# Deltanet with a two-expert router: 832 rows an expert in place of 896, the last 64 on the divided array

## The chip, the cores and the metric

The kernel runs on one core of a Trainium2 chip. The metric is device time in microseconds, the median of several runs. TensorE (PE) multiplies and transposes, VectorE (DVE) and ScalarE (ACT) read what it leaves in PSUM, GpSimd (POOL) issues the indirect DMAs, and SyncE (SP) the plain ones.

## The reference

Two blocks follow one another. The first is a linear attention with a delta rule over 4 batches, 8 heads, 768 steps and 48 channels. Its result becomes 3072 rows of 384 for a mixture of 8 experts, of which each row takes two:

```python
for t in range(S):
    y[:, :, t] = einsum('bhd,bhde->bhe', q[:, :, t], state)
    v_old = einsum('bhde,bhd->bhe', state, kt)
    state = state + bt * einsum('bhd,bhe->bhde', kt, vt - v_old)
...
noisy_logits = x @ w_gate + np.log1p(np.exp(x @ w_noise)) * noise
top2 = the two largest of 8; top2_w = their softmax
for e in range(E):                       # E = 8
    h = np.maximum(x[mask] @ w1[e], 0.0) # 384 -> 1024
    out[mask] += top2_w * (h @ w2[e])    # 1024 -> 384
```

All inputs and outputs are float32. Counted from the reference on its inputs, the eight experts get 711, 771, 789, 774, 756, 744, 807 and 792 rows.

## The kernel before

The deltanet stage routes as it goes. For every token it writes one row of 388 numbers (384 of x, and the token's number, gates and expert) twice into `rows_x`, a buffer in HBM with one part for each expert, by indirect DMAs of GpSimd (`spread`, L176). Ahead of that SP clears the first 896 rows of each part (`clear`, L171) to rows that carry the number of no token. `before` holds the running counts of rows per expert.

The expert stage takes each expert in turn (loop at L794), always with TILES = 7 tiles of 128 rows:

- SP loads all seven tiles as one DMA into `xr` (L798; two buffers, so the next expert's rows come early) and then the weights of the next expert.
- VectorE takes the token numbers and gates out of `xr` (L806, L760, L764).
- GpSimd gathers the sums so far of these tokens from the output into `sums` (L776), which waits for the scatters of the expert before.
- TensorE transposes each tile (three 128*128 transposes, L733), and VectorE copies them to `xe` (L734).
- `first` multiplies with w1: two halves of 448 rows as moving columns, eight blocks of F, three steps of the contraction each (L740), and ScalarE evicts with a Relu (L744).
- `second` multiplies tile by tile with w2: eight blocks of F accumulate 384 columns in one PSUM bank (L750). VectorE multiplies by the gate and adds to `sums` (L754), and GpSimd scatters the tile to the output (L785).

A scheduler places the instructions on each engine from their dependences, in program order with small exchanges. PSUM buffers come from a pool of eight banks that transposes, first and second products share. A float32 matmul shows as two records in the trace, a transpose as one.

After the loop a matmul of ones with `before` gives the counts (L836), VectorE reduces them to the largest (L838, L839), all engines load it into a register (`values_load`, L840), and a branch (L841) does the left-over rows, tile by tile with 128 columns, if an expert has more than TILES * 128.

Of the kernel before, what the change touches and what calls it, by code (L numbers as in the profile page):

```python
# [8 lines left out]
FP32 = mybir.dt.float32  # L9
I32 = mybir.dt.int32  # L10
ALU = mybir.AluOpType
ACTF = mybir.ActivationFunctionType
AX = mybir.AxisListType
SYNC = mybir.DependencyInfo(mybir.DependencyClass.Sync, mybir.DependencyReason.DATA)
# [1 line left out]
C = 64  # L16
DP = 64
Q = 32
TILES = 7
ROW = 384 + 4  # L20
HALF = TILES * 128 // 2


@with_exitstack
def kernel(
# [10 lines left out]
    moe_w2: bass.AP,  # L36
    out: bass.AP,
):

# [23 lines left out]
    nc = tc.nc  # L63

    B, H, S, D = q.shape
    N, DM = out.shape
    E = moe_w_gate.shape[1]
# [7 lines left out]
    KT = DM // 128  # L75
    FT = F // 128
# [62 lines left out]
    def load_weights(pool, e):  # L139
        w1e = pool.tile([128, KT, F], FP32, name="w1e")  # L140
        w2e = pool.tile([128, FT, DM], FP32, name="w2e")
        nc.sync.dma_start(out=w1e, in_=w1r[e])
        nc.sync.dma_start(out=w2e, in_=w2r[e])
        return w1e, w2e
# [23 lines left out]
    def clear(e):  # L168

        return nc.sync.dma_start(  # L170
            out=rows_x[e * N : e * N + TILES * 128].rearrange("(t p) d -> p t d", p=128),  # L171
            in_=empty[:, None, :].to_broadcast([128, TILES, ROW]),
        ).ins

    def spread(rows, slot):
# [549 lines left out]
    def ps(shape, name):  # L725
        return psum.tile(shape, FP32, name=name, tag="ps")

    moe = ctx.enter_context(tc.tile_pool(name="moe", bufs=2))

    def transposed(xr, xe, i):  # L730
        p_xt = ps([128, KT, 128], "p_xt")
        for do in range(KT):
            nc.tensor.transpose(p_xt[:, do], xr[:, i, do * 128 : (do + 1) * 128], ident)  # L733
        nc.vector.tensor_copy(xe[:, :, i * 128 : (i + 1) * 128], p_xt)  # L734

    def first(w1e, xe, hT, cols):
        for fo in range(FT):
            p_h = ps([128, cols.stop - cols.start], "p_h")
            for do in range(KT):
                nc.tensor.matmul(  # L740
                    p_h, w1e[:, do, fo * 128 : (fo + 1) * 128], xe[:, do, cols],
                    start=(do == 0), stop=(do == KT - 1),
                )
            nc.scalar.activation(hT[:, fo, cols], p_h, ACTF.Relu)  # L744

    def second(w2e, hT, i, gate, got):

        p_o = ps([128, DM], "p_o")
        for fo in range(FT):
            nc.tensor.matmul(  # L750
                p_o, hT[:, fo, i * 128 : (i + 1) * 128], w2e[:, fo],
                start=(fo == 0), stop=(fo == FT - 1),
            )
        nc.vector.scalar_tensor_tensor(  # L754
            out=got, in0=p_o, scalar=gate, in1=got, op0=ALU.mult, op1=ALU.add
        )

    def gates_of(xr, e, gate):

        nc.vector.scalar_tensor_tensor(  # L760
            out=gate, in0=xr[:, :, DM + 3], scalar=float(e - E), in1=xr[:, :, DM + 2],
            op0=ALU.is_equal, op1=ALU.mult,
        )
        nc.vector.tensor_tensor(out=gate, in0=gate, in1=xr[:, :, DM + 1], op=ALU.add)  # L764
# [9 lines left out]
    def gather(got, index, group, earlier):  # L774
        return ordered(
            nc.gpsimd.indirect_dma_start(  # L776
                out=got, out_offset=None, in_=out,
                in_offset=bass.IndirectOffsetOnAxis(ap=index, axis=0),
                bounds_check=N - 1, oob_is_err=False,
            ).ins, group, earlier,  # L780
        )

    def scatter(got, index, group, earlier):
        return ordered(
            nc.gpsimd.indirect_dma_start(  # L785
                out=out, out_offset=bass.IndirectOffsetOnAxis(ap=index, axis=0), in_=got,
                in_offset=None, bounds_check=N - 1, oob_is_err=False,
            ).ins, group, earlier,
        )

    sums = [moe.tile([128, TILES, DM], FP32, name=f"sums{i}", bufs=1) for i in range(2)]
    for got in sums:
        nc.gpsimd.memset(got, 0.0)
    for e in range(E):  # L794
        w1e, w2e = weights
        rows = slice(e * N, e * N + TILES * 128)
        xr = moe.tile([128, TILES, ROW], FP32, name="xr")
        d = nc.sync.dma_start(  # L798
            out=xr, in_=rows_x[rows].rearrange("(t p) d -> p t d", p=128)
        ).ins  # L800
        for i in written:
            tc.add_manual_dep(d, i.name, SYNC, reason="rows of all tokens")
        if e + 1 < E:
            weights = load_weights(w_odd if e % 2 == 0 else w_even, e + 1)
        index = moe.tile([128, TILES], I32, name="index")
        nc.vector.tensor_copy(index, xr[:, :, DM])  # L806
        gate = moe.tile([128, TILES], FP32, name="gate")
        gates_of(xr, e, gate)
        got = sums[e % 2]
        gathers = [  # L810
            gather(got[:, i], index[:, i : i + 1], f"out{e}", added) for i in range(TILES)
        ]
        added = []
        xe = moe.tile([128, KT, TILES * 128], FP32, name="xe")
        for i in range(TILES):
            transposed(xr, xe, i)
        hT = moe.tile([128, FT, TILES * 128], FP32, name="hT", bufs=1)
        for h0 in range(0, TILES * 128, HALF):
            first(w1e, xe, hT, slice(h0, h0 + HALF))
        for i in range(TILES):  # L820
            second(w2e, hT, i, gate[:, i : i + 1], got[:, i])
            added.append(
                scatter(got[:, i], index[:, i : i + 1], f"out{e}", gathers if i == 0 else [])
            )


    counts = moe.tile([128, E], FP32, name="counts", bufs=1)
    most = moe.tile([128, 1], FP32, name="most", bufs=1)
    most_i = moe.tile([128, 1], I32, name="most_i", bufs=1)
    place = moe.tile([128, NT], FP32, name="place", bufs=1)  # L830
    nc.gpsimd.iota(
        place, pattern=[[128, NT]], base=0, channel_multiplier=1,
        allow_small_or_imprecise_dtypes=True,
    )
    p_n = ps([128, E], "p_n")
    nc.tensor.matmul(p_n, ones, before)  # L836
    nc.vector.tensor_copy(counts, p_n)
    nc.vector.tensor_reduce(out=most, in_=counts, axis=AX.X, op=ALU.max)  # L838
    nc.vector.tensor_copy(most_i, most)  # L839
    count = nc.values_load(most_i[0:1, 0:1], min_val=0, max_val=N)  # L840
    with tc.If(count > TILES * 128):  # L841
        for e in range(E):
            with tc.tile_pool(name=f"left{e}", bufs=1) as pool:
                w1e = pool.tile([128, KT, F], FP32, name="w1l")
                w2e = pool.tile([128, FT, DM], FP32, name="w2l")
                nc.sync.dma_start(out=w1e, in_=w1r[e])
                nc.sync.dma_start(out=w2e, in_=w2r[e])
                earlier, added = added, []
                for i in range(TILES, NT):
                    r0 = e * N + i * 128  # L850
                    xr = pool.tile([128, 1, ROW], FP32, name="xrl")
                    nc.sync.dma_start(out=xr[:, 0], in_=rows_x[r0 : r0 + 128])
# [55 lines left out]
```

## Time and profile before

| | |
|---|---|
| median of 3 runs | 1134.44 us (1134.03 to 1136.22) |
| profiled execution | 1132.78 us, span 1131.1 us |
| TensorE matmul busy | 933.2 us (83%) |
| first products L740 | 291.0 us, 768 records |
| second products L750 | 290.3 us, 896 records |
| transposes L733 | 21.9 us, 168 records |
| mean granted TensorE clock | 0.825 |

Busy times are sums over the whole span. [...] A record's own duration is longer than the step to the next one, since matmuls are pipelined; the steps tell what a matmul costs in a stream.

### The profile page before, as it was taken

Reading aid. Unit: us, or ns where it says so; the run is one execution under the profiler, and the core shown is the slowest. Engines: PE = TensorE matmul, PEld = TensorE weight load, DVE = VectorE, ACT = ScalarE, POOL = GpSimd, SP = SyncE. Lnnn points to the kernel's source line nnn. Section 1 sums busy time; section 2 is a strip of 40 time slices with the busy share of each in tenths; the row PEclk is TensorE's granted clock in tenths of the full one; section 3 lists DMA queues with packets and bytes.
Section 4 is the critical chain, followed back from the end, with each engine's and each line's share of the span. In section 5 each row is a group of like instructions: output and inputs, shape, how many; then the busy total and the mean of one; then the engine's idle time right before and its main releaser. Section 6 shows DMA issues by size and latency. Waiting matters only on the chain.

```text
span 1131.1 us, 20168 instructions
## 1 busy us (share of the span) xinstructions
PE 933.2 (83%) x8670; PEld 631.0 (56%) x8670; DVE 314.1 (28%) x883; ACT 257.4 (23%) x621; POOL 239.8 (21%) x297
## 2 busy tenths in 40 slices
PE   2258147877958688827999999999999999999995
PEld 2258046777858677724565555555655555556553
DVE  1866753383664733011010020110100201102000
ACT  3353234434416242101102002011020020110200
POOL 4201112314142140223022121130221211301211
PEclk9655558675666656558999999999999999999998
DMA  5895202322121120118114241241142412301100
GB/s 106 255 369 151 42 2 65 79 45 82 29 75 33 30 72 2 57 57 297 63 36 143 77 139 31 91 156 63 48 134 76 143 29 86 106 8 37 43 21 26
DMA packets 120403, 96.34 MB, mean 85 GB/s; under 512 B 84690, under 2 KB 110350, under 8 KB 120304
## 3 DMA queue, kind: packets, MB, share of 16 engines
q1 hardware_dynamic: 109168, 66.42, 20.1%
q0 software_dynamic: 10240, 28.43, 7.4%
q8 instruction: 70, 1.15, 0.4%
q14 instruction: 29, 0.24, 0.1%
q10 hardware_dynamic: 896, 0.10, 0.1%
HBM read 61.68 MB, written 36.39 MB: 87 GB/s over the span
## 4 chain that ended last, share of the span: by engine, by line
PE 70%; DVE 11%; issue 6%; ACT 6%; another core or an unknown queue 2%; DMA 1%; POOL 1%; ACTq 1%; SPq 0%; DVEq 0%; POOLq 0%
PE p_h L740 26%; PE p_o L750 26%; PE p_y L426 3%; DVE t L348 2%; DVE part L344 2%; PE p_y L420 2%; PE p_u L485 2%; PE p_xt L446 2%; PE p_x L388 2%; ACT w L373 2%; ACT gd L304 1%; PE p_x L379 1%; PE p_xt L438 1%; PE p_b L281 1%
## 5 line engine op out<-in xcount | busy, mean ns | idle before, releaser
L740 PE MATMUL p_h<-xe,w1e 128*128 128x448 f32 x768 | 291.0, 540 | 1.9 <-DVE xe L734 1.9
L750 PE MATMUL p_o<-w2e,hT 128*128 128x384 f32 x896 | 290.3, 486 | 0.0
L750 PEld LDWEIGHTS p_o<-w2e,hT 128*128 128x128 f32 x896 | 170.2, 190 | 119.6 <-issue 3.0
L740 PEld LDWEIGHTS p_h<-xe,w1e 128*128 128x128 f32 x768 | 145.5, 190 | 143.4 <-issue 139.9
L744 ACT ACTIVATE hT<-p_h 128x448 f32<-128x448 f32 x128 | 69.5, 543 | 520.3 <-PE p_h L740 483.2
L754 DVE SCALAR_TENSOR_TENSOR sums<-p_o,gate,sums 128x384 f32<-128x384 f32 x56 | 34.6, 617 | 508.4 <-PE p_o L750 508.4
L785 POOL DMA_INDIRECT out_dram<-sums,index x56 | 55.6, 993 | 438.6 <-DVE sums L754 428.8
L176 POOL DMA_INDIRECT rows_x<-y,slot x48 | 49.8, 1038 | 90.3 <-issue 41.2
L776 POOL DMA_INDIRECT sums<-out_dram,index x56 | 56.5, 1010 | 55.2 <-issue 38.5
L348 DVE TENSOR_TENSOR t<-t,part 128x30 f32<-128x30 f32 (+9 forms) x180 | 61.2, 340 | 4.8
L344 DVE TENSOR_TENSOR part<-t 128x30 f32<-128x30 f32 (+9 forms) x180 | 60.9, 338 | 4.8
L281 PE MATMUL p_q<-qT,kT 64*64 64x64 f32 x768 | 18.8, 256 | 51.0 <-ACT qT L273 48.9
L485 PE MATMUL p_u<-v,w 64*64 64x48 f32 x768 | 43.3, 284 | 10.3 <-ACT y L433 8.9
L373 ACT COPY w<-tt 32x256 f32<-32x256 f32 x96 | 38.6, 402 | 56.8 <-DVE tt L359 55.4
L485 PEld LDWEIGHTS p_u<-v,w 64*64 64x64 f32 x768 | 40.6, 202 | 13.8 <-ACT y L433 6.8
L281 PEld LDWEIGHTS p_q<-qT,kT 64*64 64x64 f32 x768 | 16.4, 164 | 54.7 <-ACT qT L273 52.3
L426 PE MATMUL p_y<-u,qk 64*64 64x48 f32 x768 | 45.8, 298 | 0.0
L426 PEld LDWEIGHTS p_y<-u,qk 64*64 64x64 f32 x768 | 41.9, 213 | 5.3 <-issue 4.9
L515 POOL COPY wide<-st 64x384 f32<-64x384 f32 x44 | 23.0, 523 | 98.1 <-DVE st L512 82.6
L459 POOL TENSOR_TENSOR v<-v,norms 128x384 f32<-128x384 f32 x24 | 21.1, 892 | 99.3 <-DMA v<-in_v_dram 84.4
L379 PE MATMUL p_x<-tb,at 32*32 32x32 f32 x768 | 21.8, 220 | 24.0 <-DVE tb L360 22.1
L733 PE MATMUL p_xt<-ident,xr 128*128 128x128 f32 x168 | 21.9, 291 | 20.0 <-DMA xr<-rows_x 20.0
(130 smaller groups left out, 824.3 us busy)
## 6 DMA issues: line engine op xcount, KB each, us to landing
w1e<-in_moe_w_dram SPq DMA_DIRECT2D x8, 1536.0 KB
w2e<-in_moe_w_dram SPq DMA_DIRECT2D x8, 1536.0 KB
rows_x<-empty SPq DMA_DIRECT2D x8, 1358.0 KB
xr<-rows_x SPq DMA_DIRECT2D x8, 1358.0 KB
kp<-in_k_dram SPq DMA_DIRECT2D x48, 96.0 KB
qp<-in_q_dram SPq DMA_DIRECT2D x48, 96.0 KB
v<-in_v_dram SPq DMA_DIRECT2D x48, 96.0 KB
out_dram<-empty SPq DMA_DIRECT2D x1, 4608.0 KB
```

Source lines behind the costliest of these rows:

```text
L176: d = nc.gpsimd.indirect_dma_start(out=rows_x, out_offset=bass.IndirectOffsetOnAxis(ap=slot, axis=0), in_=rows, in_offset=None,).ins
L281: nc.tensor.matmul(out[rows_of[b], z, j], lhsT[rows_of[z], j, rows_of[b]], rhs(rows_of[z], j, b), start=(j == 0), stop=(j == NP - 1), skip ...
L344: nc.vector.tensor_tensor(out=part, in0=t[:, j + 1 :, j, None].to_broadcast(shape), in1=t[:, None, j, 0:j].to_broadcast(shape), op=ALU.mult,)
L348: nc.vector.tensor_tensor(out=t[:, j + 1 :, 0:j], in0=t[:, j + 1 :, 0:j], in1=part, op=ALU.add)
L373: nc.scalar.copy(w64[rows, :, cols], tt[rows])
L426: nc.tensor.matmul(p_y[b, h], qk[b, h % 2, h // 2], u[b, h], start=(c == 0 and h == 0), stop=(h == H - 1), skip_group_check=True,)
L485: nc.tensor.matmul(p_u[b, h], w64[b, h], r[b, h], start=(h == 0), stop=(h == H - 1), skip_group_check=True,)
L740: nc.tensor.matmul(p_h, w1e[:, do, fo * 128 : (fo + 1) * 128], xe[:, do, cols], start=(do == 0), stop=(do == KT - 1),)
L744: nc.scalar.activation(hT[:, fo, cols], p_h, ACTF.Relu)
L750: nc.tensor.matmul(p_o, hT[:, fo, i * 128 : (i + 1) * 128], w2e[:, fo], start=(fo == 0), stop=(fo == FT - 1),)
L776: nc.gpsimd.indirect_dma_start(out=got, out_offset=None, in_=out, in_offset=bass.IndirectOffsetOnAxis(ap=index, axis=0), bounds_check=N - ...
L785: nc.gpsimd.indirect_dma_start(out=out, out_offset=bass.IndirectOffsetOnAxis(ap=index, axis=0), in_=got, in_offset=None, bounds_check=N - ...
```

## The change

TILES becomes 6, and 64 rows more (MORE) make 832 rows an expert. The first products take two halves of 416 columns. The seventh tile has 64 rows: its transposes read 64 partitions, and its second products load 64 columns of weights. `second_half` gives the even blocks of F to the PSUM partitions 0 to 63 and the odd ones to 64 to 127, and VectorE adds the two halves to `sums` one after the other. `xr` is loaded by two DMAs, and the numbers and gates are taken in two pieces. The count of rows stands ahead of the expert loop, and its load into registers behind expert 0. The branch for left-over rows starts at the seventh tile and leaves out its first 64 rows.

```diff
-TILES = 7
+TILES = 6
+MORE = 64
+ROWS = TILES * 128 + MORE
-HALF = TILES * 128 // 2
+HALF = ROWS // 2
...
-    def transposed(xr, xe, i):
+    def transposed(xr, xe, i, rows=128):
         p_xt = ps([128, KT, 128], "p_xt")
         for do in range(KT):
-            nc.tensor.transpose(p_xt[:, do], xr[:, i, do * 128 : (do + 1) * 128], ident)
-        nc.vector.tensor_copy(xe[:, :, i * 128 : (i + 1) * 128], p_xt)
+            nc.tensor.transpose(
+                p_xt[:, do, 0:rows], xr[0:rows, i, do * 128 : (do + 1) * 128],
+                ident[0:rows, 0:rows],
+            )
+        nc.vector.tensor_copy(xe[:, :, i * 128 : i * 128 + rows], p_xt[:, :, 0:rows])
...
+    def second_half(w2e, hT, gate, got):
+
+        p_o = ps([128, DM], "p_o")
+        halves = [slice(lo, lo + MORE) for lo in (0, 64)]
+        for fo in range(FT):
+            nc.tensor.matmul(
+                p_o[halves[fo % 2]], hT[:, fo, ROWS - MORE : ROWS], w2e[:, fo],
+                start=(fo < 2), stop=(fo >= FT - 2), skip_group_check=True,
+            )
+        for half in halves:
+            nc.vector.scalar_tensor_tensor(
+                out=got[0:MORE], in0=p_o[half], scalar=gate[0:MORE], in1=got[0:MORE],
+                op0=ALU.mult, op1=ALU.add,
+            )
...
+    p_n = ps([128, E], "p_n")
+    nc.tensor.matmul(p_n, ones, before)
+    nc.vector.tensor_copy(counts, p_n)
+    nc.vector.tensor_reduce(out=most, in_=counts, axis=AX.X, op=ALU.max)
+    nc.vector.tensor_copy(most_i, most)
...
+        loads = [
+            nc.sync.dma_start(
+                out=xr[:, 0:TILES], in_=rows_x[rows].rearrange("(t p) d -> p t d", p=128)
+            ).ins,
+            nc.sync.dma_start(out=xr[0:MORE, TILES], in_=rows_x[more]).ins,
+        ]
...
-        for i in range(TILES):
-            second(w2e, hT, i, gate[:, i : i + 1], got[:, i])
+        for i, p in enumerate(rows_in):
+            if p < 128:
+                second_half(w2e, hT, gate[:, i : i + 1], got[:, i])
+            else:
+                second(w2e, hT, i, gate[:, i : i + 1], got[:, i])
...
+        if e == 0:
+            count = nc.values_load(most_i[0:1, 0:1], min_val=0, max_val=N)
...
-    with tc.If(count > TILES * 128):
+    with tc.If(count > ROWS):
```

On TensorE the end of the deltanet stage and the first expert stood in this order before (p_xt are transposes, p_h first products, p_o second products; a row counts matmuls):

```order
L591 MATMUL p_at<-r_taken,ones 128x8
L595 MATMUL p_at<-before,ones 128x32
L733 MATMUL p_xt<-ident,xr 128x128 x21
L740 MATMUL p_h<-xe,w1e 128x448 x48
L750 MATMUL p_o<-w2e,hT 128x384 x56
```

The same three rows follow for every further expert.

The same place on TensorE now:

```order
L599 MATMUL p_at<-before,ones 128x32
L818 MATMUL p_n<-before,ones 128x8
L737 MATMUL p_xt<-ident,xr 128x128 x18
L737 MATMUL p_xt<-ident,xr 128x64 x3
L747 MATMUL p_h<-xe,w1e 128x416 x48
L772 MATMUL p_o<-w2e,hT 128x384 x48
L758 MATMUL p_o<-w2e,hT 64x384 x8
```

The counting matmul p_n has come ahead of the first transposes, and eight matmuls of 64 rows stand where eight of 128 stood, right before the next expert's transposes.

On VectorE the border between experts 0 and 1 was, before, the last sums of expert 0 and then the copies of expert 1's transposes (one p_xt for each tile):

```order
L754 SCALAR_TENSOR_TENSOR sums0_6110<-p_o_6328,gate_6122,sums0_6110 128x384
L754 SCALAR_TENSOR_TENSOR sums0_6110<-p_o_6341,gate_6122,sums0_6110 128x384
L734 COPY xe_6386<-p_xt_6387 128x3x128
L734 COPY xe_6386<-p_xt_6392 128x3x128
L734 COPY xe_6386<-p_xt_6397 128x3x128
L734 COPY xe_6386<-p_xt_6402 128x3x128
```

Three more copies follow, one for each further tile.

The same border on VectorE now, with the half tile's bank p_o_6353 read twice:

```order
L776 SCALAR_TENSOR_TENSOR sums0_6118<-p_o_6340,gate_6130,sums0_6118 128x384
L763 SCALAR_TENSOR_TENSOR sums0_6118<-p_o_6353,gate_6130,sums0_6118 64x384
L741 COPY xe_6417<-p_xt_6418 128x3x128
L763 SCALAR_TENSOR_TENSOR sums0_6118<-p_o_6353,gate_6130,sums0_6118 64x384
L741 COPY xe_6417<-p_xt_6423 128x3x128
L741 COPY xe_6417<-p_xt_6428 128x3x128
L741 COPY xe_6417<-p_xt_6433 128x3x128
```

The half tile's second sum has come between the first and the second copy.

On SP the loads of expert 0's rows and expert 1's weights, and what follows them, now read as follows (TENSOR_LOAD puts the count into a register):

```order
L833 DMA xr<-rows_x 128x6x388
L836 DMA xr<-rows_x 64x388
L146 DMA w1e<-in_moe_w_dram 128x3x1024
L147 DMA w2e<-in_moe_w_dram 128x8x384
L869 TENSOR_LOAD most_i
L869 ISA x2
```

Expert 1's rows come right behind these. Before, the load of the count stood behind all of SP's DMAs; on the four other engines it stands last before and now.

## Rows read from the trace of the kernel before

**Rows 1.** Windows: expert stage; busy us and records, clock, DMA.

```profile
core 0: us, PE busy (x) PEld busy (x) DVE busy (x) ACT busy (x) POOL busy (x), PEclk, DMA share, GB/s
...
519.30:1117.20 597.90, 595.99 (x1814) 332.38 (x1813) 60.28 (x128) 69.53 (x128) 108.55 (x109) 1.00 0.24 81
```

**Rows 2.** Windows: expert 0's transposes, a border, then first and second products.

```profile
514.74:519.80 5.06, 5.04 (x22) 4.86 (x23) 4.05 (x10) 0.00 (x0) 3.06 (x3) 0.50 1.03 394
...
591.74:594.47 2.73, 2.46 (x22) 2.22 (x21) 2.53 (x6) 0.00 (x0) 0.98 (x1) 1.00 0.54 85
594.47:630.65 36.18, 36.18 (x96) 18.35 (x97) 1.76 (x6) 8.15 (x15) 7.07 (x7) 1.00 0.33 109
630.65:666.77 36.12, 36.12 (x113) 21.23 (x112) 3.71 (x6) 0.54 (x1) 5.96 (x6) 1.00 0.21 76
```

**Rows 3.** Timeline, border of experts 0 and 1: start, us, instruction, count [idle <-releaser].

```profile
590.77 1.13 PE L750 MATMUL p_o<-w2e,hT 128*128 128x384 f32 x3
...
591.74 2.46 PE L733 MATMUL p_xt<-ident,xr 128*128 128x128 f32 x21
...
591.94 0.62 DVE L754 SCALAR_TENSOR_TENSOR sums<-p_o,gate,sums 128x384 f32<-128x384 f32 x1 [4.54 <-PE p_o L750]
592.48 3.33 DVE L734 COPY xe<-p_xt 128x384 f32<-128x384 f32 x7
...
594.47 1.77 PE L740 MATMUL p_h<-xe,w1e 128*128 128x448 f32 x4 [0.27 <-DVE xe L734]
```

**Rows 4.** Waits of TensorE: us in total, times, longest.

```profile
PE p_h L740 <- DVE xe L734: 1.9, 7, 0.3
```

**Rows 5.** Instruction groups: count, busy us, mean ns, idle before.

```profile
L750 PE MATMUL p_o<-w2e,hT 128*128 128x384 f32 x896 | 290.3, 486 | 0.0
...
L744 ACT ACTIVATE hT<-p_h 128x448 f32<-128x448 f32 x128 | 69.5, 543 | 520.3 <-PE p_h L740 483.2 <-DMA sums<-out_dram,index 30.4 <-issue 6.8
```

**Rows 6.** Timeline: products of the deltanet stage on column halves.

```profile
471.81 0.91 PE L420 MATMUL p_y<-wide,qT 128*64 128x96 f32 x8
```

**Rows 7.** Line L420 from 470 to 482: ns, min, median and max.

```profile
L420 PE MATMUL p_y<-wide,qT x32: 367/368/423, 471.8 to 481.0; 128*64 128x96 f32 x32
```

**Rows 8.** Windows: inside those L420 products, and inside 64*64 products of L281.

```profile
471.80:472.35 0.55, 0.55 (x8) 0.54 (x8) 0.00 (x0) 0.43 (x1) 0.00 (x0) 0.50 0.00 0
446.34:446.75 0.41, 0.41 (x32) 0.41 (x36) 0.38 (x2) 0.33 (x1) 0.37 (x2) 1.00 0.00 0
```

**Rows 9.** Timeline: expert 0's transposes.

```profile
514.76 4.71 PE L733 MATMUL p_xt<-ident,xr 128*128 128x128 f32 x21 [19.98 <-DMA xr<-rows_x]
```

**Rows 10.** Line L733, all transposes: ns, min, median and max.

```profile
L733 PE MATMUL p_xt<-ident,xr x168: 272/273/445, 514.8 to 1044.1; 128*128 128x128 f32 x168
```

**Rows 11.** Timeline: changes between whole and divided array at full clock.

```profile
441.65 0.55 PE L438 MATMUL p_xt<-ident,y 128*128 128x128 f32 x3
442.13 0.55 PE L503 MATMUL p_s<-u,kp 64*64 64x48 f32 x20
...
444.37 1.09 PE L271 MATMUL p_t<-ident,qp 128*128 128x128 f32 x8
```

**Rows 12.** Timeline of SP's loads at the start of the expert stage.

```profile
508.42 0.38 SPq L798 DMA_DIRECT2D xr<-rows_x  x1
...
509.98 9.88 SPq L798 DMA_DIRECT2D xr<-rows_x  x2
```

**Rows 13.** The page's DMA issues: the load of an expert's rows.

```profile
xr<-rows_x SPq DMA_DIRECT2D x8, 1358.0 KB
```

**Rows 14.** Timeline of GpSimd: the last scatter.

```profile
1118.07 0.98 POOL L785 DMA_INDIRECT out_dram<-sums,index  x1 [4.18 <-DVE most L838]
```

**Rows 15.** Window after it.

```profile
1119.10:1131.10 12.00, 0.00 (x0) 0.00 (x0) 0.00 (x0) 0.00 (x0) 0.00 (x0) 0.56 0.06 13
```

**Rows 16.** Waits of SP's queue.

```profile
SPq L840 <- DVE most_i L839: 150.4, 1, 150.4
```

**Rows 17.** Line L841, the branch, on TensorE: ns.

```profile
L841 PEldq COMPARE_BRANCH  x1: 3512/3512/3512, 1119.2 to 1119.2; - x1
```

More of the change, by code (lines that the diff above doesn't have):

```diff
@@ L170, in clear @@
         return nc.sync.dma_start(
-            out=rows_x[e * N : e * N + TILES * 128].rearrange("(t p) d -> p t d", p=128),
-            in_=empty[:, None, :].to_broadcast([128, TILES, ROW]),
+            out=rows_x[e * N : e * N + (TILES + 1) * 128].rearrange("(t p) d -> p t d", p=128),
+            in_=empty[:, None, :].to_broadcast([128, (TILES + 1), ROW]),
         ).ins
@@ L789, in scatter @@
         )
-    sums = [moe.tile([128, TILES, DM], FP32, name=f"sums{i}", bufs=1) for i in range(2)]
+    counts = moe.tile([128, E], FP32, name="counts", bufs=1)
+    most = moe.tile([128, 1], FP32, name="most", bufs=1)
+    most_i = moe.tile([128, 1], I32, name="most_i", bufs=1)
+    p_n = ps([128, E], "p_n")
[3 more added lines that the diff above has]
+    nc.vector.tensor_copy(most_i, most)
+    sums = [moe.tile([128, TILES + 1, DM], FP32, name=f"sums{i}", bufs=1) for i in range(2)]
     for got in sums:
         nc.gpsimd.memset(got, 0.0)
+    rows_in = [128] * TILES + [MORE]
     for e in range(E):
@@ L796 @@
         rows = slice(e * N, e * N + TILES * 128)
[L797 to L802, printed above, removed]
+        more = slice(rows.stop, rows.stop + MORE)
+        xr = moe.tile([128, TILES + 1, ROW], FP32, name="xr")
+        loads = [
[4 more added lines that the diff above has]
+        ]
@@ L803 @@
+        for d in loads:
+            for i in written:
+                tc.add_manual_dep(d, i.name, SYNC, reason="rows of all tokens")
         if e + 1 < E:
             weights = load_weights(w_odd if e % 2 == 0 else w_even, e + 1)
[L805 to L808, printed above, removed]
+        index = moe.tile([128, TILES + 1], I32, name="index")
+        gate = moe.tile([128, TILES + 1], FP32, name="gate")
@@ L809 @@
+        for p, t in ((128, slice(0, TILES)), (MORE, slice(TILES, TILES + 1))):
+            nc.vector.tensor_copy(index[0:p, t], xr[0:p, t, DM])
+            gates_of(xr[0:p, t], e, gate[0:p, t])
         got = sums[e % 2]
         gathers = [
-            gather(got[:, i], index[:, i : i + 1], f"out{e}", added) for i in range(TILES)
+            gather(got[0:p, i], index[0:p, i : i + 1], f"out{e}", added)
+            for i, p in enumerate(rows_in)
         ]
         added = []
-        xe = moe.tile([128, KT, TILES * 128], FP32, name="xe")
@@ L815 @@
-        for i in range(TILES):
-            transposed(xr, xe, i)
-        hT = moe.tile([128, FT, TILES * 128], FP32, name="hT", bufs=1)
-        for h0 in range(0, TILES * 128, HALF):
-            first(w1e, xe, hT, slice(h0, h0 + HALF))
-        for i in range(TILES):
-            second(w2e, hT, i, gate[:, i : i + 1], got[:, i])
+        xe = moe.tile([128, KT, ROWS], FP32, name="xe")
+        for i, p in enumerate(rows_in):
+            transposed(xr, xe, i, p)
+        hT = moe.tile([128, FT, ROWS], FP32, name="hT", bufs=1)
@@ L822 @@
+        for h0 in range(0, ROWS, HALF):
+            first(w1e, xe, hT, slice(h0, h0 + HALF))
+        for i, p in enumerate(rows_in):
+            if p < 128:
+                second_half(w2e, hT, gate[:, i : i + 1], got[:, i])
+            else:
+                second(w2e, hT, i, gate[:, i : i + 1], got[:, i])
             added.append(
-                scatter(got[:, i], index[:, i : i + 1], f"out{e}", gathers if i == 0 else [])
+                scatter(got[0:p, i], index[0:p, i : i + 1], f"out{e}", gathers if i == 0 else [])
@@ L824 @@
             )
-    counts = moe.tile([128, E], FP32, name="counts", bufs=1)
-    most = moe.tile([128, 1], FP32, name="most", bufs=1)
-    most_i = moe.tile([128, 1], I32, name="most_i", bufs=1)
+        if e == 0:
+            count = nc.values_load(most_i[0:1, 0:1], min_val=0, max_val=N)
     place = moe.tile([128, NT], FP32, name="place", bufs=1)
@@ L834 @@
     )
[L835 to L840, printed above, removed]
-    with tc.If(count > TILES * 128):
+    nc.vector.memset(place[0:MORE, TILES : TILES + 1], float(N))
+    with tc.If(count > ROWS):
         for e in range(E):
```

## The prediction

> **What bounds the kernel now.** I read the page first for where the time lies, then the windows of one expert, then the timeline of one border between two experts, and last the places where the trace already shows the forms of instruction that the change brings in. [...] One expert is three stretches [rows 2]: 36.18 us of first products (96 records, two for each of 48 matmuls), 36.12 us of second products (112 records for 56 matmuls, so 5.16 us a tile), and 2.73 us of border, in which 21 transposes run and TensorE then waits 0.27 us for VectorE (594.47 less 591.74 + 2.46), seven times in the program [rows 3]. No load, eviction or scatter ends a wait of TensorE inside the stage except 1.9 us on xe [rows 4]. So a column that goes away in L740 or L750 is time that goes away, and all else is to be counted at the borders, the start and the end.
>
> **First products.** 448 columns become 416. Per record 36.18/96 = 0.377 us, or 0.84 ns a column; the second products give 36.12/112 = 0.3225 us for 384 columns, 0.84 ns again, so time goes by columns. 36.18 x 32/448 = 2.58 us an expert, **-20.7 us** for eight. ScalarE's eviction (543 ns [rows 5]) runs once in six records (2.1 us) and stays hidden.
>
> **Second products.** Six full tiles keep their 5.16 us. The seventh has 64 rows: eight matmuls that each load 64 columns of weights and write 64 partitions, even blocks to the lower half, odd ones to the upper. The trace has this very form: L420, 128*64, whose inner loop also alternates the halves. Eight records of 96 columns take 0.91 us, the last 0.37, so (0.91 - 0.37)/7 = 0.077 us a record, at clock 0.50 [rows 6 to 8]. One after the other at that clock they would take 0.16 us: the transposes of expert 0 at clock 0.50 need (4.71 - 0.445)/20 = 0.213 us for 128 columns [rows 9, 10], 1.67 ns a column, times 96. Two therefore run at once. That this holds at the upper clock is seen in 64*64 products at clock 1.00: 32 records of 64 columns in 0.41 us, 0.013 each where 0.054 would be due alone [rows 8]; four at a time there, with the same number of partitions streamed as two of 128. So the half tile costs 16 x 0.3225/2 = 2.58 us in place of 5.16: 2.58 us an expert, **-20.6 us**. Bounds: nothing (no overlap), and the 20.6.
>
> **Change of form.** Between 128*128 and a divided array the next load begins only near the end of the last matmul. At full clock the last of three transposes starts at 441.65 + 0.55 - 0.273 = 441.93 and the 64*64 products at 442.13, 0.20 us later where the step inside one form is (2.46 - 0.273)/20 = 0.109; going back, eight transposes take 1.09 us, some 0.05 more than at 0.109 a step [rows 3, 10, 11]. So about 0.15 us a change. Four changes come with each expert: into the half tile, out of it, and into and out of the 64-row transposes. Only the first stands on the path, since the other three lie in the border, where TensorE waits for VectorE: **+1.2 us** (8 x 0.15; 0.4 to 2.8). [...]
>
> **The border.** Before, the last second product starts at 590.77 + 1.13 - 0.486 = 591.41 [rows 3, 5]; VectorE's sum follows at 591.94, the first xe copy at 592.48, the others every (3.33 - 0.55)/6 = 0.464 us, and L740 starts at 594.47, just when the fourth copy ends (592.48 + 3 x 0.464 + 0.55 = 594.42) [rows 3]. 416 columns need four tiles as well. In the new order the second sum of the half tile stands between the first and the second copy, on the path. A sum before a copy takes 0.54 us there (592.48 - 591.94), so every border grows by about 0.54 us, seven times: **+3.8 us** (0.3 to 0.9 a border). TensorE's transposes, over by some 2.9 us after the last second product, stay ahead of the copies that end at 3.6.
>
> **Start of the stage.** Expert 0's first load goes from 1,358 to 1,164 KB (six tiles of seven). TensorE starts 6.34 us after SP issues it; 194 KB at the 394 GB/s of that stretch is 0.5 us [rows 2, 9, 12, 13]. What is won runs at the lower clock if that rises when it did, at 519.8, so **-0.4 us** (0 to -0.9). VectorE has three more small operations ahead of its copies (0.17 us each), hidden because the transposes come at 0.64 us a tile there. The counting matmul and its three VectorE operations move into the 20 us in which TensorE waits for that load.
>
> **The count.** Only SP's TENSOR_LOAD moves forward, behind the loads of expert 1's weights; on the four other engines it still stands last. It waits for one VectorE cast that is early now. Behind it on SP stands expert 1's xr, issued at 509.98 before, in 9.88 us together with the next one, and used at 591.74 [rows 3, 12]: some 70 us of room, so nothing.
>
> **The end.** After the last scatter (1118.07 + 0.98) no engine works for 12.0 us [rows 14, 15]. The last expert's two sums follow one another with no copy between: the scatter comes 0.65 us later (0.618 and a wait). Against that TensorE, ScalarE and SP no longer wait for the count until 1118.3 (SP waited 150.4 us for it [rows 16]), and TensorE's branch of 3.5 us [rows 17] may run beside matmuls; but GpSimd, whose path goes through the scatter, gains little. **+0.4 us** (-0.4 to +0.7).
>
> **Sum.** -20.7 - 20.6 + 1.2 + 3.8 - 0.4 + 0.4 = -36.3 us. The profiled execution took 1132.78 us (span 1131.1): 1096.5. The median shown, 1134.44, lies 1.66 above it, so the forecast is 1098.1 us, say **1098**. With the bounds of the terms (-40 to -31) and the spread of the runs shown it is 1094 to 1104.
>
> **Rivals.**
> (a) The halves do not overlap for 384 columns, because two streams of 128 partitions are needed at the upper clock, of which L420's rows say nothing (0.50). For it: no row has this form at 1.00. Against: the 64*64 rows. The 20.6 are not won: 1118.7 us. 5%.
> (b) The clock falls at the borders. They hold 2.6 us of work on the divided array, transposes, and 0.8 us of waiting instead of 0.27. After expert 0's long wait the clock stayed at 0.50 for 5.06 us, through 21 transposes [rows 2]; if each of seven borders cost the same, 5.06 x 0.5 = 2.5 us each is 17.7 us: 1116. Against: seven borders of today keep 1.00, with 2.46 us of transposes in them. 8%. [...]
> (c) Slower: the branch for rows beyond the tiles is taken. It decides from 833 rows of one expert, where 897 were needed. Then 8 x 18 tiles of 128 rows follow, at 5.16 us for their second products alone: over 740 us more, above 1840. Against: counting the reference's routing on its inputs gives 711 to 807 rows an expert. 0.5%.
> (d) Both (a) and (b): 38.3 us lost of 36.3 won, 1136. 0.5%.
>
> **How the numbers follow.** The forecast's case has 83%, (a) 5%, (b) 8%, and 4% are left for (c), (d) and costs that I do not see. Of the first case some 3 in 83 fall outside its own range widened to 1093 to 1107, which so holds 8 in 10; (a) and (b) stay outside it. Within 0.2% (2.3 us, about what a measurement of this kernel can tell from no change) lie (d) and half of what I do not see: 2%; slower are (c) and the other half: 2%; the rest, with (a) and (b), is faster: 96%.
>
> **What would show it.** Right: L747 records every 0.349 us; L758 records in pairs that take 2.6 us an expert; a period from one expert's first product to the next of 70.6 us for 75.0; TensorE idle 0.7 to 1.0 us before L747 behind VectorE; clock 1.00 from 519 us on; the second sum between two xe copies. Wrong: L758 at 0.32 us a record one after another (a), a stretch of 0.50 inside the stage (b), any xrl instruction at all (c), or TensorE waiting for DMA at a border.

## The result, and the profile after

The changed kernel takes 1100.97 us (median of 4 runs, 1097.86 to 1106.57) where the kernel before took 1135.33 us beside it (median of 4, 1134.03 to 1139.32): a ratio of 0.970, with a 95% interval from 0.965 to 0.975. The forecast was 1098 us, in a range of 1093 to 1107. Its profiled execution took 1099.18 us with a span of 1097.5 us, 33.6 us under the span before.

First the page's costliest groups of the changed kernel: line, engine, operation, tiles and shapes, count, then busy us and mean ns of one, then the idle time before them and its releaser.

```profile
L747 PE MATMUL p_h<-xe,w1e 128*128 128x416 f32 x768 | 270.3, 513 | 6.3 <-DVE xe L741 6.3
L772 PE MATMUL p_o<-w2e,hT 128*128 128x384 f32 x768 | 249.0, 486 | 0.0
```

Six tiles of 128 rows are left for L772 (768 records for the 896 of [rows 5]), and L747 now sits idle for 6.3 us behind VectorE's xe, where [rows 4] had 1.9: three times as much, still seven times in the program.

Then the windows that answer to [rows 1, 2]: expert 0's transposes in two pieces, the expert stage from its first product to its last matmul, and of the border its transposes, of expert 1 the first products, the six tiles and the half tile. Columns as in [rows 1].

```profile
514.57:518.19 3.62, 3.60 (x17) 3.62 (x18) 3.04 (x11) 0.00 (x0) 2.06 (x3) 0.50 1.01 396
518.19:518.75 0.56, 0.56 (x6) 0.33 (x4) 0.56 (x2) 0.00 (x0) 0.56 (x1) 1.00 1.06 370
518.76:1081.90 563.14, 556.82 (x1813) 315.11 (x1811) 64.87 (x155) 66.18 (x128) 107.47 (x109) 1.00 0.26 85
...
586.16:589.58 3.42, 2.52 (x23) 2.21 (x21) 3.23 (x7) 0.00 (x0) 0.93 (x1) 1.00 0.67 182
589.58:623.21 33.63, 33.62 (x96) 18.35 (x97) 1.69 (x9) 7.75 (x15) 6.99 (x7) 1.00 0.31 104
623.21:654.26 31.05, 31.05 (x97) 18.05 (x95) 3.09 (x5) 0.52 (x1) 4.98 (x5) 1.00 0.23 83
654.26:656.99 2.73, 2.73 (x17) 1.06 (x16) 0.62 (x1) 0.00 (x0) 0.98 (x1) 1.00 0.07 27
```

First products go from 36.18 to 33.63 us an expert, second products from 36.12 to 31.05 + 2.73 = 33.78, the stretch from the first transpose to the next first product from 2.73 to 3.42 [rows 2]. The granted clock, given as a share of the full one, is 1.00 from the second row on, in the border's row too, and so from the first product to the last.

The timeline of the border between experts 0 and 1, TensorE first, then VectorE; the line of 583.81 is the second pair of the half tile's sixteen records by itself. Each line has its start, its us, the instruction with its count, and in brackets the idle time before it with the releaser.

```profile
583.02 0.49 PE L772 MATMUL p_o<-w2e,hT 128*128 128x384 f32 x1
583.44 2.80 PE L758 MATMUL p_o<-w2e,hT 128*64 128x384 f32 x16
...
583.81 0.49 PE L758 MATMUL p_o<-w2e,hT 128*64 128x384 f32 x2
...
586.17 2.51 PE L737 MATMUL p_xt<-ident,xr 128*128 128x128 f32 x21
589.59 0.62 PE L747 MATMUL p_h<-xe,w1e 128*128 128x416 f32 x1 [0.91 <-DVE xe L741]
...
586.29 0.61 DVE L763 SCALAR_TENSOR_TENSOR sums<-p_o,gate,sums 64x384 f32<-64x384 f32 x1 [2.12 <-PE p_o L758]
586.82 0.54 DVE L741 COPY xe<-p_xt 128x384 f32<-128x384 f32 x1
587.39 0.62 DVE L763 SCALAR_TENSOR_TENSOR sums<-p_o,gate,sums 64x384 f32<-64x384 f32 x1
588.04 2.42 DVE L741 COPY xe<-p_xt 128x384 f32<-128x384 f32 x5
...
660.41 0.62 PE L747 MATMUL p_h<-xe,w1e 128*128 128x416 f32 x1 [0.90 <-DVE xe L741]
```

Sixteen records of the half tile take 2.80 us where one alone takes 0.486 us. They start in pairs, one record of each half with 0.007 us between them; all fifteen steps together are 2.80 - 0.49 = 2.31 us, 0.154 us a record on average, about half of the 0.3225 us of a whole tile's [rows 2]. The last of them starts at 583.44 + 2.80 - 0.49 = 585.75 and the next expert's first product at 589.59, 3.84 us later; before, it was 594.47 - 591.41 = 3.06 [rows 3, 5]. From one expert's first product to the next it is 660.41 - 589.59 = 70.82 us, for 75.03 before. On VectorE the second half sum stands between the first and the second copy, as forecast, but the steps around it are 0.57 and 0.65 us, where 0.464 stood.

Last the end: the last half tile on TensorE, the last scatter, and what GpSimd's queue does behind the overflow branch (count, ns of one as min/median/max, start of the first and of the last).

```profile
1079.21 2.80 PE L758 MATMUL p_o<-w2e,hT 128*64 128x384 f32 x16
...
1083.61 0.92 POOL L807 DMA_INDIRECT out_dram<-sums,index  x1 [2.41 <-DVE sums L763]
...
L879 POOLq EVENT_SEMAPHORE  x4: 17/42/43, 1088.9 to 1091.2; - x4
L879 POOLq COMPARE_BRANCH  x1: 53/53/53, 1085.1 to 1085.1; - x1
...
L879 POOLq INC_SWDGE_SEM  x1: 1170/1170/1170, 1091.3 to 1091.3; - x1
```

And of the kernel before, its last second products and the same rows of GpSimd's queue:

```profile
1109.56 7.58 PE L750 MATMUL p_o<-w2e,hT 128*128 128x384 f32 x23
...
L841 POOLq EVENT_SEMAPHORE  x4: 17/43/43, 1124.1 to 1124.3; - x4
L841 POOLq COMPARE_BRANCH  x1: 53/53/53, 1119.5 to 1119.5; - x1
```

GpSimd takes its branch at 1085.1 and runs the first instruction behind it at 1088.9, 3.9 us later (before: 4.5). But then four semaphore instructions that took 0.2 us before take 2.3 us. Single records show where: 2.115 us lie between the first and the second of them, and in that gap one packet of 8192 bytes comes on an instruction queue (1089.56 to 1089.92). The last second product starts at 1079.21 + 2.80 - 0.49 = 1081.53, the span ends at 1097.5: 15.9 us. Before, it started at 1109.56 + 7.58 - 0.49 = 1116.65 and the span ended at 1131.1: 14.4 us.

The start of the stage, before and then now: the first product before, and of the changed kernel the issue of the first load of expert 0's rows on SP and the transposes that wait for it.

```profile
519.26 1.19 PE L740 MATMUL p_h<-xe,w1e 128*128 128x448 f32 x2
```

```profile
507.84 0.38 SPq L833 DMA_DIRECT2D xr<-rows_x  x1
...
514.59 4.12 PE L737 MATMUL p_xt<-ident,xr 128*128 128x128 f32 x19 [19.36 <-DMA xr<-rows_x]
```

The first transpose stands 6.75 us behind the load's issue, where it was 514.76 - 508.42 = 6.34 [rows 9, 12]; the first product, at 518.76, stands 10.92 us behind it, where it was 519.26 - 508.42 = 10.84. The start itself has so become 0.1 us longer. That the first product comes 0.5 us sooner is due to the load's issue, 507.84 for 508.42, that is, to the deltanet stage ahead of it.

The account, from starts of first products and of last second products in the two traces (forecast in brackets). All products of the eight experts with their changes of form: -40.1 us (-40.1). Seven borders, each 0.78 us longer: +5.5 (+3.8). Start of the stage: +0.1 (-0.4). Deltanet stage: -0.6 (0). End: +1.5 (+0.4). The sum is -33.6 (-36.3).

### The profile page after: what moved, and what is told of

Its sections match the earlier page's. It is cut to its first block, busy times and chain, and to the rows that moved or that the text cites. A ratio compares the mean times of both kernels' runs of the same rounds, so it can differ in the third digit from the quotient of the medians.

```text
span 1097.5 us, 20220 instructions
## 1 busy us (share of the span) xinstructions
PE 889.9 (81%) x8670; PEld 609.6 (56%) x8670; DVE 320.2 (29%) x916; ACT 253.9 (23%) x621; POOL 238.5 (22%) x297
## 5 line engine op out<-in xcount | busy, mean ns | idle before, releaser
L747 PE MATMUL p_h<-xe,w1e 128*128 128x416 f32 x768 | 270.3, 513 | 6.3 <-DVE xe L741 6.3
L772 PE MATMUL p_o<-w2e,hT 128*128 128x384 f32 x768 | 249.0, 486 | 0.0
L747 PEld LDWEIGHTS p_h<-xe,w1e 128*128 128x128 f32 x768 | 145.3, 190 | 127.0 <-issue 119.7
L772 PEld LDWEIGHTS p_o<-w2e,hT 128*128 128x128 f32 x768 | 145.9, 190 | 102.2 <-issue 2.5
L751 ACT ACTIVATE hT<-p_h 128x416 f32<-128x416 f32 x128 | 66.2, 517 | 491.5 <-PE p_h L747 475.9
L776 DVE SCALAR_TENSOR_TENSOR sums<-p_o,gate,sums 128x384 f32<-128x384 f32 x48 | 29.7, 618 | 449.8 <-PE p_o L772 449.8
L489 PE MATMUL p_u<-v,w 64*64 64x48 f32 x768 | 39.7, 269 | 9.0 <-ACT y L437 7.1
L489 PEld LDWEIGHTS p_u<-v,w 64*64 64x64 f32 x768 | 37.2, 186 | 11.7 <-ACT y L437 6.6
L737 PE MATMUL p_xt<-ident,xr 128*128 128x128 f32 (+1 forms) x168 | 21.8, 285 | 19.4 <-DMA xr<-rows_x 19.4
```

The costliest lines, as they stand in the source:

```text
L489: nc.tensor.matmul(p_u[b, h], w64[b, h], r[b, h], start=(h == 0), stop=(h == H - 1), skip_group_check=True,)
L747: nc.tensor.matmul(p_h, w1e[:, do, fo * 128 : (fo + 1) * 128], xe[:, do, cols], start=(do == 0), stop=(do == KT - 1),)
L772: nc.tensor.matmul(p_o, hT[:, fo, i * 128 : (i + 1) * 128], w2e[:, fo], start=(fo == 0), stop=(fo == FT - 1),)
```

## The experiments

Eight runs were made, in two groups of four, each group on one chip; the second group holds the changed kernel once more, unaltered, and the half tile first for a second time. On the chip of the first group the deltanet stage, which all kernels share, was shorter and varied more (the second expert's first product less one period is 500.3 us in one trace, 518.8 in the changed kernel's first): the kernel before took 1111.81 us there (median of 11, 1100.70 to 1121.08). So stretches of the expert stage are compared across chips, and times only as ratios to the kernel before on the same chip.

**One half of the array for all eight blocks.** The overlap is taken away, and with it the second half sum.

```
-        halves = [slice(lo, lo + MORE) for lo in (0, 64)]
+        halves = [slice(0, MORE)]
...
-                p_o[halves[fo % 2]], hT[:, fo, ROWS - MORE : ROWS], w2e[:, fo],
-                start=(fo < 2), stop=(fo >= FT - 2), skip_group_check=True,
+                p_o[halves[0]], hT[:, fo, ROWS - MORE : ROWS], w2e[:, fo],
+                start=(fo == 0), stop=(fo == FT - 1), skip_group_check=True,
```

> All eight blocks of the 64-row tile go to the lower half of the array, one after the other, and one sum is left instead of two. Theory (the gain of the half tile is the overlap of the two halves): 16 records at 0.3225 us a record, so the half tile's first to last record grows from 2.31 to 4.84 us in every expert; the border without the second sum falls from 3.83 to about 3.07 us; period of an expert 72.6 us for 70.8; time 1113 us (1099.2 + 7 x 1.76 + 1.9). Rival (a matmul with 64 columns of weights is cheaper by itself): half tile stays at 2.3 us, border 3.07, time 1094.

Measured: ratio 0.983 (0.977 to 0.989), 1092.19 us. The timeline of its second border:

```profile
637.00 5.37 PE L758 MATMUL p_o<-w2e,hT 128*64 128x384 f32 x16
642.31 2.51 PE L737 MATMUL p_xt<-ident,xr 128*128 128x128 f32 x21
644.94 0.62 PE L747 MATMUL p_h<-xe,w1e 128*128 128x416 f32 x1
...
642.42 0.61 DVE L763 SCALAR_TENSOR_TENSOR sums<-p_o,gate,sums 64x384 f32<-64x384 f32 x1 [4.69 <-PE p_o L758]
642.95 3.12 DVE L741 COPY xe<-p_xt 128x384 f32<-128x384 f32 x7
```

The half tile takes 5.37 us for 2.80, so the two halves do run at once in the changed kernel, at a granted clock of 1.00 too (the window from 654.26 to 656.99 in the section above). The border is 644.94 - (637.00 + 5.37 - 0.49) = 3.06 us, as before the change: with one sum nothing stands between the copies. The period is 72.61 us for 70.82. The second half of the array so gains 2.57 us an expert and gives 0.78 back at the border.

**Blocks in turn.** Four blocks for the lower half, then four for the upper: the same matmuls, the same two sums, another order.

```
-                p_o[halves[fo % 2]], hT[:, fo, ROWS - MORE : ROWS], w2e[:, fo],
-                start=(fo < 2), stop=(fo >= FT - 2), skip_group_check=True,
+                p_o[halves[fo // 4]], hT[:, fo, ROWS - MORE : ROWS], w2e[:, fo],
+                start=(fo % 4 == 0), stop=(fo % 4 == 3), skip_group_check=True,
```

> Blocks 0 to 3 of F go to the lower half of the array and 4 to 7 to the upper, in that order, instead of alternating. Theory (matmuls start in program order, so two halves overlap only where neighbours alternate): seven of eight steps inside a half at 0.32 us, half tile 4.5 us from first to last record for 2.31; period 73.0 us; time about 1117. Rival (each half has a queue of its own): half tile 2.3 us, time 1099.

Measured: ratio 0.971 (0.964 to 0.979), 1080.82 us; the half tile takes 3.66 us from its first record to its last, which is between the two. The timeline of the half tile, then windows that cut it in three (columns: window and us, PE busy and records, PEld busy and records, clock, DMA share, GB/s), L758 alone:

```profile
628.72 4.14 PE L758 MATMUL p_o<-w2e,hT 128*64 128x384 f32 x16
```

```profile
628.72:630.06 1.34, 1.34 (x4) 0.60 (x5) 1.00 0.00 0
630.06:631.40 1.34, 1.34 (x9) 0.72 (x8) 1.00 0.13 48
631.40:632.79 1.39, 1.39 (x6) 0.41 (x3) 1.00 0.26 95
```

Records are counted in each window that they touch. Four of the lower half run alone, then lower and upper side by side, then the upper alone, 4.14 us in all. The first upper record starts at 630.067, beside the fifth of the eight lower ones, so TensorE had begun upper work with three lower records still to start. In turn the two halves overlap by themselves for a few records only; in alternating order all sixteen run in pairs, in 2.80 us. The period, 72.15 us, is 1.33 longer than the changed kernel's, which is the 4.14 - 2.80 of the half tile.

**The half tile first.** It becomes the first of the seven second products, so that a whole tile with one sum stands last.

```
-        for i, p in enumerate(rows_in):
+        for n, i in enumerate([TILES, *range(TILES)]):
+            p = rows_in[i]
...
-                scatter(got[0:p, i], index[0:p, i : i + 1], f"out{e}", gathers if i == 0 else [])
+                scatter(got[0:p, i], index[0:p, i : i + 1], f"out{e}", gathers if n == 0 else [])
```

> The half tile's second products come first of the seven tiles, so a full tile with one sum stands at the border. Theory (two sums of the half tile stand on the path at the border and at the end): border from last second product to first first product 3.05 us as in the kernel before, for 3.83; the half tile's two changes of form now both stand on the path, 0.1 us each; period 70.1 us for 70.8; end 0.65 us shorter; 1099.2 - 4.9 - 0.6 = 1093.7 us for the profiled execution. Rival (the border is held by the changes of form and the transposes, not by VectorE): border stays at 3.6 to 3.8 us, time 1099 to 1100.

Measured: ratio 0.961 (0.956 to 0.966), 1067.79 us. Timeline of one expert and the border behind it:

```profile
604.22 2.80 PE L758 MATMUL p_o<-w2e,hT 128*64 128x384 f32 x16
606.95 31.23 PE L772 MATMUL p_o<-w2e,hT 128*128 128x384 f32 x96
638.02 2.46 PE L737 MATMUL p_xt<-ident,xr 128*128 128x128 f32 x21
640.75 0.62 PE L747 MATMUL p_h<-xe,w1e 128*128 128x416 f32 x1 [0.27 <-DVE xe L741]
...
638.22 0.62 DVE L776 SCALAR_TENSOR_TENSOR sums<-p_o,gate,sums 128x384 f32<-128x384 f32 x1 [4.54 <-PE p_o L772]
638.75 2.87 DVE L741 COPY xe<-p_xt 128x384 f32<-128x384 f32 x6
```

TensorE's wait is 0.27 us again, as in [rows 3], and both half sums now run beside a whole tile's matmuls. The border is 640.75 - (606.95 + 31.23 - 0.49) = 3.06 us for 3.84. The period falls by 0.58 us only, to 70.24, since two changes of form stand on the path in place of one (+0.20 in single records). The second half sum, and nothing else of the half tile, made the border longer.

**The upper half summed first.** What is left open is why that sum costs 0.78 us and not the 0.54 of the forecast.

```
-        for half in halves:
+        for half in halves[::-1]:
```

> The changed kernel with one edit: of the two half sums after the half tile's products, the one that reads the upper half of the accumulator (partitions 64 to 127) is taken first, the one that reads the lower half second. In the changed kernel the copy behind the first sum starts 0.534 us after it, the copy behind the second 0.651 us after it, and the second sum itself lasts 0.62 us where the first lasts 0.61. Theory A: the extra 0.12 us belongs to the sum that reads partitions 64 to 127 and writes 0 to 63. Then the slow step moves to the first copy (0.65 us behind its sum), the second one's step is 0.53, and the border stays at 3.8 us. Theory B: it belongs to whichever sum comes second, because that one must wait for the first on the same engine (it reads what the first wrote). Then all steps stay as in the changed kernel: 0.53 behind the first sum, 0.57 to the second, 0.65 behind it, border 3.83 us. By either the period stays within 0.1 us of 70.82.

Measured: one run, 1101.73 us. Timeline of its first border on VectorE, then TensorE's first product:

```profile
589.38 0.62 DVE L763 SCALAR_TENSOR_TENSOR sums<-p_o,gate,sums 64x384 f32<-64x384 f32 x1 [2.12 <-PE p_o L758]
590.03 0.56 DVE L741 COPY xe<-p_xt 128x384 f32<-128x384 f32 x1
590.51 0.60 DVE L763 SCALAR_TENSOR_TENSOR sums<-p_o,gate,sums 64x384 f32<-64x384 f32 x1
591.03 2.40 DVE L741 COPY xe<-p_xt 128x384 f32<-128x384 f32 x5
...
592.56 0.62 PE L747 MATMUL p_h<-xe,w1e 128*128 128x416 f32 x1 [0.78 <-DVE xe L741]
```

The step of 0.65 us has moved to the first sum, with the upper half. The lower half's sum, now second, stands 0.48 us behind a copy and 0.52 before the next: together 0.54 more than one copy step of 0.464, which is the forecast's figure to the hundredth. So theory A holds: at these borders a copy starts some 0.08 us before the copy ahead of it has ended (0.55 us every 0.464), as does the lower half's sum behind a copy (590.51 for 590.03 + 0.56), and the sum that reads partitions 64 to 127 and writes 0 to 63 does not take part in that. It starts 0.03 us after the copy ahead of it has ended (587.39 for 586.82 + 0.54 in the changed kernel), and the copy behind it starts 0.03 us after its own end (590.03 for 589.38 + 0.62). In the second place it loses 0.1 us on each side, in the first place only behind it: the border falls to 592.56 - 588.85 = 3.71 us, 0.12 less, where theory A had said that it stays.

**The count last.** The counting matmul, its three VectorE operations and the loads of the count go back behind the experts.

```
-    p_n = ps([128, E], "p_n")
-    nc.tensor.matmul(p_n, ones, before)
...
-        if e == 0:
-            count = nc.values_load(most_i[0:1, 0:1], min_val=0, max_val=N)
...
+    p_n = ps([128, E], "p_n")
+    nc.tensor.matmul(p_n, ones, before)
...
+    count = nc.values_load(most_i[0:1, 0:1], min_val=0, max_val=N)
```

> The count and its load into registers go back behind the expert loop; all else as changed. Theory (GpSimd's path through the last scatter sets the end, not the count): period 70.8 us as it is; the end from last second product to the end of the span, 15.97 us, moves by -2 to +1 with where code is fetched; time 1097 to 1100. Rival (the count first hides TensorE's branch and the wait for the count): the end grows by 3 us or more, time 1102 or above.

Measured: ratio 0.977 (0.970 to 0.983), 1082.5 us; period and border as in the changed kernel (70.82 and 3.83 us), last second product to the end 17.26 us for 15.93, between the two expectations. Timeline of the end, and GpSimd behind the branch:

```profile
1054.84 0.61 DVE L763 SCALAR_TENSOR_TENSOR sums<-p_o,gate,sums 64x384 f32<-64x384 f32 x1 [2.12 <-PE p_o L758]
1055.38 0.14 DVE L873 COPY counts<-p_n 128x8 f32<-128x8 f32 x1
1055.55 0.62 DVE L763 SCALAR_TENSOR_TENSOR sums<-p_o,gate,sums 64x384 f32<-64x384 f32 x1
...
1056.28 0.15 DVE L875 CAST most_i<-most 128x1 int32<-128x1 f32 x1
1056.45 0.92 POOL L807 DMA_INDIRECT out_dram<-sums,index  x1 [2.47 <-DVE most_i L875]
```

```profile
L877 POOLq EVENT_SEMAPHORE  x4: 17/43/43, 1062.3 to 1065.4; - x4
L877 POOLq COMPARE_BRANCH  x1: 53/53/53, 1057.9 to 1057.9; - x1
```

The count itself costs 0.06 us here: last second product to last scatter is 1056.45 - 1054.31 = 2.14 us for 2.08. The rest of the 1.33 us is GpSimd waiting behind its branch, 4.3 us for 3.9 and then 2.9 for 2.1, here where all engines branch between 1057.2 and 1057.9; in the changed kernel SP, ScalarE and TensorE branch at 940.8, 1049.7 and 1080.9, well ahead of GpSimd (1085.1). Taking the count first so is worth some 1.3 us in this pair of traces (the three other traces with the count first and both sums last have 15.6 to 16.3 us there); whether the earlier branches of the other engines are the reason was not tried by itself. The second stall is not the early count's doing, since it is longer here.

**Three kernels on one chip: the changed one, the half tile first, and shifted code.** The last takes the half tile first and adds to the overflow branch, which isn't taken, sixteen memsets on GpSimd that never run. They only move what stands behind the branch in GpSimd's code.

```
+    pad = moe.tile([1, 1], FP32, name="pad", bufs=1)
     with tc.If(count > ROWS):
+        for _ in range(16):
+            nc.gpsimd.memset(pad, 0.0)
```

> The changed kernel itself, unaltered, on the same chip as the two that follow, so that their times can be set against it there. Expected: period of an expert 70.82 us, border 3.83, last matmul to the end 15.9, as in its first profile; ratio to the kernel before 0.970, between 0.965 and 0.977.

> The changed kernel with the half tile's second products taken first of the seven instead of last, once more, on the same chip as the changed kernel itself. Expected: period 70.24 us for 70.82, border 3.05 us for 3.83, last matmul to the end 14.9 us for 15.9; 8 x 0.58 + 0.5 = 5 us under the changed kernel, ratio to the kernel before about 0.965. Rival: the stage's gain is given back elsewhere (start or end), and the two kernels come out within 2 us of each other.

> The kernel with the half tile first, and in the overflow branch, which is not taken, sixteen small memsets on GpSimd: nothing of them is executed, but GpSimd's instructions behind the branch lie sixteen and more places further on in its code. In all five profiles of the kernel with 832 rows GpSimd stalls twice behind the branch: 3.3 to 4.3 us up to its first instruction there, and then again 2.1 to 2.9 us between the first and the second, in which one further packet of 8192 bytes comes on an instruction queue; in the kernel before the second gap was 0.07 us. Theory: the first instruction behind the branch is the last of a block of 8192 bytes, so that the next block must be fetched after it has run; shifted, the second gap falls below 0.2 us, the last matmul to the end takes 12.5 to 13.0 us for 14.9, and the kernel is some 2 us under the one with the half tile first alone. Rival: the second gap is a wait for something else (the last scatter's landing, another engine); then it stays at 2.0 to 2.5 us and the end at 14.9.

Measured, beside the kernel before at 1136.41 us (median of 11): the changed kernel 1102.13 us, ratio 0.971 (0.967 to 0.976); half tile first 1097.92, 0.967 (0.963 to 0.971); half tile first with shifted code 1097.08, 0.967 (0.963 to 0.971). Against the changed kernel the two are at 0.9956 (0.992 to 0.999) and 0.9951 (0.992 to 0.998), taken from the means of six runs of each and by resampling them, a gain of half a per cent; against each other at 0.999 (0.996 to 1.003), which tells nothing. By their medians the half tile first is 4.2 us under the changed kernel, where 5 were forecast. The changed kernel's trace shows the 70.82, 3.83 and 15.9 us of its first one again. GpSimd behind the branch, first with the half tile first, then with shifted code:

```profile
L880 POOLq EVENT_SEMAPHORE  x4: 17/43/43, 1082.8 to 1085.1; - x4
```

```profile
L881 POOLq EVENT_SEMAPHORE  x5: 17/43/43, 1090.6 to 1090.9; - x5
```

The second stall is gone: the semaphore instructions (one more for the memsets) stand within 0.3 us, where they took 2.3, and 5 instruction packets of 8192 bytes follow the branch, where 6 follow it in the changed kernel's trace. The last second product to the end takes 12.8 us for 14.8, as the theory had it. That is one trace of the shifted code, beside those of the unshifted, which have the second stall (2.1 to 2.9 us). These 2 us show in the traces; in the median they drown in the spread of the runs (9.8 us from lowest to highest). This version is under both kernels, and by its trace it is the best of those run: 70.24 us an expert and 12.8 us behind the last second product, for 70.82 and 15.9.

## Why the prediction was right, and where it was off

- **First products, second products, overlap, change of form: right, in sum and in parts.** L747 records stand 33.63/96 = 0.350 us apart (0.349 forecast), and the half tile's pairs take the time of one record. Rival (a) falls: its work in one half costs 5.37 us for 2.80. The four changes of form were counted right, one on the path of each expert, and that one has the size forecast: the first half record starts 583.44 - 583.02 = 0.416 us behind the last whole one and the second pair 0.373 us behind the first, where 0.3225 is a step, so 0.094 + 0.051 = 0.145 us for 0.15. The forecast had read the two parts, 0.09 and 0.05 us, at two different changes; here both come at one. The first load of half weights begins near the end of the last whole matmul, as the forecast had it: it starts at 583.435, 0.07 us ahead of that record's end (583.020 + 0.486 = 583.506), where between the last two whole matmuls the load starts 0.48 us ahead of such an end (582.700 for 583.184).
- **The clock: right.** 1.00 in all rows of the stage, so rival (b) falls: 2.5 us of transposes and 0.9 us of waiting at a border do not bring it down. Nor did transposes alone hold it down at the start: at expert 0 of the changed kernel TensorE has stood for 19.4 us, runs nothing but transposes from 514.59 on, and the clock goes from 0.50 to 1.00 at 518.19, 0.57 us ahead of the first product (windows above).
- **The border: mechanism right, term mis-sized.** "A sum before a copy takes 0.54 us there" took the price from the sum of 128 partitions in the kernel before, which overlaps with the copy behind it (592.48 for 591.94 + 0.62). That price holds for the lower half (0.54 in the run with the upper half first). The upper half's sum stood in the second place, without overlap on either side: 0.78 us, inside the bounds given (0.3 to 0.9), and 7 x 0.24 = 1.7 us in all.
- **The start: the number by luck, the step wrong.** The forecast let TensorE start 0.5 us sooner because the load has 194 KB less. The first transpose stands 0.4 us later behind the load's issue instead (6.75 us for 6.34, and 6.79 to 6.96 in the eight other traces with 832 rows, where the 64 rows are a second load right behind). Why is not shown; no run changed the loads alone. From there to the first product it is 4.17 us for 4.50, with the last transposes at 1.00 where all ran at 0.50 before. The -0.5 us by which the first product came sooner is the deltanet stage, for which the forecast's sum has no term: the load's issue lies 0.6 us earlier in this execution. It lies anywhere between 480.4 and 514.6 us in the eight others, so those 0.6 us cannot be called a gain of the change.
- **The count: right.** SP's early load of the count holds nobody up: no wait of TensorE in the stage ends on a DMA. The count's early place is worth some 1.3 us at the end.
- **The end: the larger of the two steps that failed.** +1.5 us for +0.4, beyond its bound of +0.7. The 0.65 us of the second sum came as forecast (last second product to last scatter 2.08 us for 1.42). "GpSimd, whose path goes through the scatter, gains little" looked at what it gains and not at what its own code costs behind the branch. There 2.1 us came in that the trace before has at 0.07, and 1.2 us went elsewhere (first stall 3.86 for 4.55, the last two instructions some 0.5 us shorter). The run with shifted code shows, in its one trace, that the 2.1 us hang on where the instructions lie (all five within 0.3 us there), which no row of the kernel before could show.
- **The branch was not taken**, so rival (c) falls; (d), which is (a) and (b) together, falls with them.

The border missed by 1.7 us, the end by 1.1 and the start by 0.5; less the 0.6 us of the deltanet stage, that is the 2.7 us by which the profiled run (1099.18) missed the sum's 1096.5. The median lies 1.8 us above the profiled run.

## What to carry to other kernels

Split work for TensorE was cheap on TensorE here (2.80 us for 5.37) and dear where its parts are added (0.78 us more at each of seven borders): price the extra additions at the place where they stand, and give a part that needs several of them a place in the middle of a stage, where the next part's matmuls cover them, not the last place before a border. Work for two halves of the array is better alternated in the program than put in turn: 2.80 us for 4.14 here. Before a span's end counts as fixed, look at the gaps between single instructions behind a branch: here they took 2.3 us, and 0.3 in the run whose code lay elsewhere.

## What the runs showed of the hardware

- VectorE's copies of 0.55 us stood every 0.464 us at the borders, each over its neighbour by about 0.08 us. A sum with its accumulator in partitions 64 to 127 and its result in 0 to 63 did not overlap on either side: a gap of 0.03 us ahead and behind (587.39 and 588.04 in the changed kernel), 0.1 us lost on each. Whether reading the upper partitions or crossing to the lower ones does it was not tried.
- With the blocks in turn, matmuls for the upper half of the array started ahead of ones still to come for the lower: the first upper record began at 630.067 with three of eight lower ones still to start.
- Behind the branch that jumps over the left-over rows' code, GpSimd stood for 4.5 us in the kernel before and for 3.3 to 4.3 us with 832 rows. With unshifted code it then stood for 2.1 to 2.9 us more, for 0.07 in the kernel before; with shifted code its five instructions there were within 0.3 us. In the changed kernel's trace a packet came 0.6 us after the first instruction (1089.56 for 1088.95), and the second instruction 1.1 us after the end of that packet (1091.06 for 1089.92). That the first instruction is the last of its block of code was the theory that foretold the shift's effect; the block's bounds themselves are in no row.
- In the changed kernel, after 19.4 us of standing, 3.6 us of fp32 transposes alone at a granted clock of 0.50 (514.57 to 518.19) were followed by 1.00, before the first product at 518.76; in the run with the upper half first so were 3.65 us of them (517.66 to 521.31). In the kernel before the clock rose behind the first product: at 519.81, for 519.26.
